# Reordering the seams of a Conformer block on one core: feed-forward work between queries and scores, softmax sums behind the values, two copies on VectorE

## The chip, the cores and the metric

The kernel runs on one core of a Trainium2 chip. The metric is the device time of one execution in microseconds (us), taken as the median of several executions. A kernel is set beside times of the kernel before on the same chip; some of these times are carried over from an earlier batch of runs. TensorE multiplies matrices, VectorE and ScalarE do elementwise work, GpSimd small jobs, and SyncE issues transfers. The profile writes them PE (with PEld for loading weights), DVE, ACT, POOL and SP.

## The reference

One Conformer block on two sequences of 4000 tokens, 512 features, bfloat16, cut to what matters here:

```python
h = _layernorm(x);   x1 = x + 0.5 * (_silu(h @ w_ff1_a) @ w_ff1_b)      # feed-forward 1, hidden 2048
h = _layernorm(x1);  q, k, v = h @ w_q, h @ w_k, h @ w_v
p = _softmax(einsum('btd,bsd->bts', q, k) * scale)                       # 4000 x 4000, one head of 512
x2 = x1 + einsum('bts,bsd->btd', p, v) @ w_o
h = _layernorm(x2) @ w_pw1;  h = h[..., :D] * _sigmoid(h[..., D:])       # gate
dc = depthwise_3_taps(h, dw);  dc = (dc - mean) / sqrt(var + 1e-05)      # mean, var over all tokens
x3 = x2 + _silu(dc) @ w_pw2
x4 = x3 + 0.5 * (_silu(_layernorm(x3) @ w_ff2_a) @ w_ff2_b)              # feed-forward 2
return _layernorm(x4)
```

## The kernel before

The tokens are cut into 16 chunks of 508 (the last of each sequence 444), each into four tiles of 127. The program is a list of stages: feed-forward 1 over all chunks, attention over all chunks with most of the convolution beside it, what is left of the convolution, feed-forward 2. Every engine runs its instructions in the order in which they are written; a wait is put in wherever a buffer is not ready. In `lags` wait pieces of work that TensorE does later (`pop` runs the oldest). Eight PSUM banks are used as two rings of four, S and Y. A bank is never read by two engines at once: the second reader waits for the first (`excl`).

The seam between feed-forward 1 and attention (DC is 4):

```python
for dc in range(DC):
    if dc == DC - 1:
        self.pop(1)              # a last piece of feed-forward 1
        old -= 1
    self.q_group(0, 0, dc)       # 4 matmuls, then a copy: ScalarE for even dc, VectorE for odd
# ... attention follows: scores of the first key tile need all four parts of the queries
```

The end of attention for the last chunk, and the convolution work that fills its layer norm:

```python
self.pop(3)
self.sums_direct(last % 2)       # 8 one-column matmuls on the split softmax sums, then 1/x on VectorE
self.pop(1)                      # the last values: 4 matmuls of 32 rows; then copy_o: output copies
# ...
self.conv_b(tail, DC - 3)
fill = [None, lambda: gates.append(self.conv_a(tail, DC - 3)), lambda: self.conv_b(tail, DC - 2),
        lambda: gates.append(self.conv_a(tail, DC - 2))]

def prepare(ti):
    self.project(last, ti)       # 4 matmuls on the output copies, then the residual on VectorE
    if ti == 2:
        gate("POOL")
    if fill[ti]:
        fill[ti]()
for ti in self.ln_tiles(last, ..., prepare, ("ACT", "ACT", "DVE", "DVE")):
    ...                          # cut: last gate of the convolution
gate("DVE")
drains = [self.depthwise(tail - 1, self.KEEP)]
for k in range(2):
    self.transpose_pair(k, 1, ("ACT", "DVE")[k], ybank(), last)
drains.append(self.depthwise(tail - 1, DC - 2))
```

The seam to feed-forward 2:

```python
finish(DC - 1, between)          # depthwise results of the last channel group; copies are put off
self.conv_shift(DC - 1)
self.swish(0, 3)
copy_away()                      # two copies out of PSUM, on ScalarE
# ... cut: weights
for cc in range(DC):
    self.swish(1, cc)            # ScalarE; TensorE's next 12 matmuls need them
self.pw2_x(0, all_t[2:], banks[2:])
self.pw2(0, all_t, banks, False)
x = [(ps[0:TILE, :], b_ps) for ps, b_ps in banks]
for ti in self.ln_tiles(0, ..., ("ACT", "ACT", "DVE", "DVE"), x):   # statistics on VectorE
    pass
# ... cut: pw2 of the second chunk, transposes of the first, then feed-forward 2
```

## Time and profile before

| | before |
|---|---|
| time, median of 3 runs | 2040.97 us (2040.7 to 2040.99) |
| span of the profiled execution | 2037.1 us |
| TensorE busy | 2028.9 us, all of the span |
| VectorE, ScalarE, GpSimd busy | 53%, 37%, 5% |
| TensorE's waits that the profile names | 2.0 us |
| granted TensorE clock | 1.00 |

Read it as a kernel whose only expensive thing is TensorE. VectorE at 53% is no limit on the average; it can matter only for a microsecond or two where one stage turns into the next. The change works on three such seams. Its lines are in the prediction.

### The profile page before, as it was taken

The numbers are of one execution on the slowest core, as the hardware profiler recorded it, in microseconds if no ns is written. First come the engines' busy times: TensorE is split into PE (matmuls) and PEld (weight loads), VectorE is DVE, ScalarE is ACT, GpSimd is POOL, SyncE is SP. The second block draws the span as 40 slices with busy tenths as digits, with TensorE's granted clock in tenths as the row PEclk, the third lists the DMA queues.
The fourth block names the chain that finished last, engine by engine and source line by source line (L and its number), as shares of the span: only waits on it lengthen the run. The fifth ranks groups of instructions, "written<-read, shape, count | busy, mean of one in ns | idle before, by whom it ended". The sixth has DMA issues, their size and how long they took to land.

```text
span 2037.1 us, 24581 instructions
## 1 busy us (share of the span) xinstructions
PE 2028.9 (100%) x9682; PEld 1030.5 (51%) x9682; DVE 1081.5 (53%) x2187; ACT 743.7 (37%) x1277; POOL 107.6 (5%) x235
## 2 busy tenths in 40 slices
PE   9999999999999999999999999999999999999998
PEld 5555555554444444445444444444455555555555
DVE  4234443334556667666766676667674443434433
ACT  3433333333333333333333333333345443443433
POOL 1000000000000000000000000000011000000000
PEclk9999999999999999999999999999999999999999
DMA  8122245420101111114421111111143111111111
GB/s 189 49 62 62 54 102 124 96 70 19 16 16 27 25 32 26 27 26 94 106 57 23 26 29 32 24 27 26 44 135 93 32 32 42 32 32 42 29 34 38
DMA packets 253122, 104.43 MB, mean 51 GB/s; under 512 B 193412, under 2 KB 252487, under 8 KB 252999
## 3 DMA queue, kind: packets, MB, share of 16 engines
q1 hardware_dynamic: 252321, 102.44, 21.6%
q8 instruction: 78, 1.28, 0.3%
q14 instruction: 45, 0.37, 0.1%
q10 hardware_dynamic: 678, 0.34, 0.1%
HBM read 33.77 MB, written 23.34 MB: 28 GB/s over the span
## 4 chain that ended last, share of the span: by engine, by line
PE 99%; ACT 0%; DVE 0%; issue 0%; POOL 0%; DVEq 0%
PE s L512 56%; PE y L512 42%; ACT work L562 0%; DVE wff L1215 0%; PE y L540 0%; ACT keys L562 0%; POOL work L1224 0%; DVE work L559 0%; DVE work L876 0%; PE y L527 0%; DVE wff L1102 0%; DVE work L1222 0%; ACT xt L562 0%; DVE work L835 0%; DVE work L1229 0%
## 5 line engine op out<-in xcount | busy, mean ns | idle before, releaser
L562 ACT ACTIVATE work<-s 128x508 bf16<-128x508 f32 (+3 forms) x1060 | 621.7, 587 | 1211.5 <-PE s L512 1207.1
L512 PE MATMUL s<-work,wff 128*128 128x508 bf16 (+4 forms) x2640 | 628.3, 369 | 0.8 <-ACT work L562 0.4
L512 PE MATMUL s<-work,keys 128*128 128x508 bf16 (+1 forms) x2048 | 516.6, 374 | 0.1
L512 PE MATMUL y<-work,keys 128*128 128x508 bf16 (+2 forms) x2048 | 503.9, 373 | 0.0
L512 PE MATMUL y<-wff,work 128*127 128x512 bf16 (+1 forms) x2000 | 501.4, 378 | 0.0
L959 DVE TENSOR_TENSOR work<-work 128x508 f32<-128x508 f32 (+2 forms) x496 | 334.4, 674 | 281.6 <-ACT work L562 280.8
L512 PEld LDWEIGHTS s<-work,wff 128*128 128x128 bf16 x2640 | 252.6, 98 | 277.0 <-issue 4.7
L512 PEld LDWEIGHTS y<-wff,work 128*127 128x127 bf16 x2000 | 274.4, 137 | 170.9
L512 PEld LDWEIGHTS s<-work,keys 128*128 128x128 bf16 x2048 | 199.4, 98 | 232.0 <-DVE work L876 0.6
L512 PEld LDWEIGHTS y<-work,keys 128*128 128x128 bf16 (+1 forms) x2048 | 193.6, 97 | 233.1 <-issue 6.2
L758 DVE SCALAR_TENSOR_TENSOR xt<-y,xt 127x512 bf16<-127x512 f32 x125 | 77.7, 682 | 364.0 <-PE y L512 364.0
L512 PE MATMUL s<-work 128*127 128x512 bf16 (+4 forms) x775 | 196.9, 378 | 1.2 <-DVE work L1333 1.2
L624 DVE BATCH_NORM_STATS2 work<-xt 127x6 f32<-127x512 bf16 x311 | 195.2, 676 | 5.2 <-DMA xt<-in_x_dram 4.9
L631 POOL TENSOR_TENSOR work<-work 127x4 f32<-127x4 f32 (+1 forms) x76 | 76.5, 1007 | 1129.4 <-DVE work L629 1129.4
L512 PEld LDWEIGHTS s<-work 128*127 128x127 bf16 (+2 forms) x775 | 94.8, 124 | 75.6 <-issue 4.0
L644 DVE TENSOR_SCALAR work<-xt,work 127x512 bf16<-127x512 bf16 x309 | 111.4, 406 | 27.4 <-POOL work L631 23.2
L758 DVE SCALAR_TENSOR_TENSOR xt<-s,xt 127x512 bf16<-127x512 f32 x55 | 38.0, 691 | 148.7 <-PE s L512 148.7
L758 DVE SCALAR_TENSOR_TENSOR xt<-s,work,xt 127x512 bf16<-127x512 f32 x64 | 48.0, 750 | 30.9 <-PE s L512 30.3
L1113 DVE SCALAR_TENSOR_TENSOR wff<-wff,s 128x508 bf16<-128x508 f32 (+1 forms) x57 | 38.7, 678 | 41.5 <-PE s L512 41.3
L562 ACT ACTIVATE wff<-s 128x508 f32<-128x508 f32 (+1 forms) x67 | 39.5, 591 | 53.5 <-PE s L512 53.4
L562 ACT ACTIVATE work<-keys,work 128x508 bf16<-128x508 bf16 (+1 forms) x68 | 52.3, 774 | 0.4 <-DVE work L1229 0.2
L1194 POOL COPY wff<-wff 128x1 bf16<-128x1 bf16 x56 | 10.4, 187 | 637.8 <-DVE wff L1113 635.0
(92 smaller groups left out, 413.0 us busy)
## 6 DMA issues: line engine op xcount, KB each, us to landing
keys<-keysd SPq DMA_DIRECT2D x62, 128.0 KB, 2.3
keysd<-work SPq DMA_DIRECT2D x14, 448.0 KB, 3.2
out_dram<-work SPq DMA_DIRECT2D x14, 448.0 KB, 3.2
dcvd<-wff SPq DMA_DIRECT2D x48, 127.0 KB, 1.9
keys<-dcvd SPq DMA_DIRECT2D x12, 508.0 KB, 4.9
xt<-in_x_dram SPq DMA_DIRECT2D x13, 448.0 KB, 4.8
wff<-in_w_ff_a_dram SPq DMA_DIRECT2D x15, 256.0 KB, 5.2
work<-work SPq DMA_TRANSPOSE x208, 2.5
```

What stands on the lines that cost most here:

```text
L512: self.S.op("PE", lambda e: e.matmul(out, lhsT, rhs, start=start, stop=stop, **kw), reads=reads, writes=[bank], inc=stop if inc is None el ...
L562: return self.S.op("ACT", lambda e: e.activation(out, in_, func, **kw), reads=reads, writes=writes)
L624: self.S.op("DVE", lambda e: e.bn_stats(self.st[sl][:, ti, 0:6], x), reads=[b_x], writes=[self.b_st[sl][ti]])
L631: S.op("POOL", lambda e: e.tensor_tensor(out=self.rs[sl][:, 0:n], in0=self.mv[sl][:, 0:n, 1], in1=self.neghalf[0:TILE, 0:n], op=ALU.pow), ...
L644: self.S.op("DVE", lambda e: e.tensor_scalar(out, x, self.mv[sl][:, ti, 0:1], self.rs[sl][:, ti:ti + 1], ALU.subtract, ALU.mult), reads=[b ...
L758: self.S.op("DVE", lambda e: e.scalar_tensor_tensor(out=self.XT[g][rows], in0=ps[rows], scalar=scalar, in1=self.XT[g][rows], op0=ALU.mult, ...
L959: S.op("DVE", lambda e, p=p, n=n, acc=acc: e.tensor_tensor(out=acc, in0=acc, in1=self.P[p][0:n, 0:W], op=ALU.add), reads=[self.b_P[p], sel ...
L1113: self.S.op("DVE", lambda e: e.scalar_tensor_tensor(out=out, in0=th, scalar=1.0, in1=ps[:, 0:W], op0=ALU.add, op1=ALU.mult), reads=[b_ps, ...
L1194: S.op("POOL", lambda e: e.tensor_copy(self.G[gs][:, jj, 0:1], self.G[gp][:, jj, CHUNK:CHUNK + 1]), reads=[self.b_G[gp][jj]], writes=[self ...
```

## The change

Its intent is to take single waits away from TensorE at the seams: more work between the last query group and the scores that need it; sums where their operands are long ready; the first tile's projection early, so that its layer norm starts early; and two copies moved to an idle VectorE so that ScalarE reaches the swishes sooner.

```diff
-                lambda: self.act(self.dcv[t][cc][:, 0:W], ps[:, 0:W], AF.Copy, [b_ps], [self.b_dcv[t][cc]]))
+                lambda eng="ACT": self.away(eng, self.dcv[t][cc][:, 0:W], ps[:, 0:W], b_ps, [self.b_dcv[t][cc]]))
 ...
         for dc in range(DC):
-            if dc == DC - 1:
-                self.pop(1)
-                old -= 1
             self.q_group(0, 0, dc)
+        self.pop(1)
+        old -= 1
 ...
         self.pop(3)
+        self.pop(1)
         self.sums_direct(last % 2)
-        self.pop(1)
 ...
-        self.conv_b(tail, DC - 3)
-        fill = [None, lambda: gates.append(self.conv_a(tail, DC - 3)), ...
+        fill = [lambda: self.conv_b(tail, DC - 3), lambda: gates.append(self.conv_a(tail, DC - 3)), ...
 ...
-            if fill[ti]:
-                fill[ti]()
+            fill[ti]()
 ...
-        def copy_away():
+        def copy_away(eng="ACT"):
             while copies:
-                copies.pop(0)()
+                copies.pop(0)(eng)
 ...
         self.swish(0, 3)
-        copy_away()
+        copy_away("DVE")
```

More of the change, by code (lines that the diff above doesn't have):

```diff
@@ L1457, in gate @@
             gates.pop(0)(eng)
-        fill = [None, lambda: gates.append(self.conv_a(tail, DC - 3)), lambda: self.conv_b(tail, DC - 2),
+        fill = [lambda: self.conv_b(tail, DC - 3), lambda: gates.append(self.conv_a(tail, DC - 3)), lambda: self.conv_b(tail, DC - 2),
                 lambda: gates.append(self.conv_a(tail, DC - 2))]
```

## The prediction

> **What bounds the kernel now.** I read the page first: what share of the span has TensorE, and at what clock.
>
> ```profile
> span 2037.1 us, 24581 instructions
> ## 1 busy us (share of the span) xinstructions
> PE 2028.9 (100%) x9682; PEld 1030.5 (51%) x9682; DVE 1081.5 (53%) x2187; ACT 743.7 (37%) x1277; POOL 107.6 (5%) x235
> ...
> PE 99%; ACT 0%; DVE 0%; issue 0%; POOL 0%; DVEq 0%
> ```
>
> TensorE is busy in all of the span, the granted clock reads 9 in all 40 slices, and the chain that ended last is TensorE for 99%. The change removes no matrix multiply, so only time in which TensorE stands still can be won. The list of TensorE's waits says how much there is of that:
>
> ```profile
> PE s L512 <- DVE work L1333: 1.2, 1, 1.2
> PE s L512 <- ACT work L562: 0.4, 1, 0.4
> PE y L540 <- ACT work L562: 0.2, 1, 0.2
> PE s L512 <- DVE work L559: 0.2, 1, 0.2
> ```
>
> That is 2.0 us in all, 1.6 of it at the start of the program, which the change doesn't touch. But ends of matmuls are modelled and overlap, so short stops hide in "busy". They show in the timeline as a distance between starts that is too long: in the steady stretches a 508- or 512-column matmul follows the last after 0.216 us (eight of 508 columns read 1.89 us, which is 7 x 0.216 plus a last one of 0.38). I looked for longer steps at the three places of the change. First, between the last feed-forward and the first scores (columns: start, duration, engine, line, operation, tiles, count, then idle time and releaser):
>
> ```profile
> 452.17 0.81 PE L512 MATMUL y<-wff,work 128*127 128x512 bf16 x3
> 452.82 1.03 PE L512 MATMUL s<-work 128*128 128x508 bf16 x4
> 453.68 2.19 PE L512 MATMUL s<-work,keys 128*128 128x508 bf16 x8
> ...
> 453.88 0.69 DVE L876 CAST work<-s 128x508 bf16<-128x508 f32 x1 [1.69 <-PE s L512]
> ```
>
> Eight score matmuls take 2.19 instead of 1.89 us. The fourth needs the last quarter of the queries, whose cast ends only at 453.88 + 0.69 = 454.57. So 0.30 us is lost here.
>
> Second, the end of attention:
>
> ```profile
> 1510.65 3.16 PE L512 MATMUL y<-work,keys 128*128 128x444 bf16 x16
> 1513.65 0.74 PE L512 MATMUL s<-work 128*127 128x1 bf16 x8
> 1514.32 0.37 PE L512 MATMUL y<-work,keys 32*128 32x444 bf16 x4
> ```
>
> The eight one-column sums, which wait for VectorE's split of the sums (its last instruction runs from 1513.53 to 1513.76), stand before the last four value matmuls.
>
> Third, the start of the second feed-forward (ScalarE's, VectorE's and TensorE's timelines, one after another):
>
> ```profile
> 1541.16 1.00 ACT L562 ACTIVATE keys<-y 128x444 bf16<-128x444 f32 x2
> 1542.05 2.90 ACT L562 ACTIVATE work<-keys,work 128x508 bf16<-128x508 bf16 x4
> ...
> 1541.78 0.70 DVE L624 BATCH_NORM_STATS2 work<-s 127x6 f32<-127x512 f32 x1 [1.37 <-PE s L512]
> ...
> 1542.91 2.96 PE L512 MATMUL y<-work 128*127 128x512 bf16 x12
> ```
>
> ScalarE copies two convolution results (1.00 us), then makes four swishes (2.90), and TensorE's twelve matmuls of the second chunk go at their pace: 2.96 us instead of 11 x 0.216 + 0.38 = 2.76. The transposes after them wait for ScalarE's normalizations (TensorE idle 0.25 us before 1546.35) and its copy out of a bank. Before its first statistics VectorE stands idle for 1.37 us.
>
> **What the Trainium skill says.** "TensorE: Matmul & The Clock Gate", in the section on 56 against 53.3 ns, gives N/2.4 + 2.5 ns per warm matmul, 216 ns for 512 columns; the trace agrees (0.216). "TensorEngine Tiling (Array Packing)", Key Properties, says that a change of tiling mode drains TensorE. The trace agrees: from the first of the four 32-row matmuls to the next work (1514.32 to 1514.62) pass 0.30 us, where one 444-column step takes 0.188. The change keeps two mode changes, so this cost stays. "ScalarE: Activation LUTs", What ACT_TABLE_LOAD costs, gives 186 ns + 0.833 ns per element, 93 more for each pointer operand, and an overlap of 93: a swish of 508 with two pointers would start every 0.70 us, as it does here. "VectorE: DVE Perf Modes", errata table, gives 120 + N cycles for a copy out of PSUM, 0.65 us for 508; the trace has 0.69 for such a cast, and I use that.
>
> **Part 1, feed-forward work between queries and scores.** The three matmuls at 452.17 move behind the fourth query group. That group then starts at 452.17, its cast 0.65 us earlier (453.23 to 453.92), while the scores still start at 453.68 and their fourth matmul at 453.68 + 3 x 0.216 = 454.33. The cast is done by then with 0.4 us to spare, so the stop goes: **-0.30 us**. The order of pops behind it is the same, so nothing is given back.
>
> **Part 2, the sums behind the values; the first tile's projection first.** Before, from the end of the 16 value matmuls (1510.65 + 16 x 0.188 = 1513.65) to the convolution's matmuls at 1514.62 is 0.97 us. After: mode change in 0.09 (what I found as the extra step at such places), the four matmuls with their drain 0.30, then eight sums without a wait at about 0.06 each, 0.48, then about 0.03: 0.90. So **-0.08 us**, give or take 0.05. The projection now comes straight after the sums, about 1514.55, and needs the output copies; the copies of the first 127 columns start when the values end, about 1514.11 (before, at 1514.71 on ScalarE and 1514.75 on VectorE), and the four of each engine take 1.10 and 1.28 us; by their sizes the first on each should be done by about 1514.45 and the second by about 1514.65; the third and fourth matmul need the second ones, at 1514.98 and 1515.2. No stop. Its residual waits for the reciprocal behind VectorE's four copies (1514.14 + 1.28 + 0.18, about 1515.6) and for its own matmuls (about 1515.6): equal. It starts 0.85 us earlier than before, which relieves the first two normalizations, but the fourth tile still follows its own projection, and the next stops of TensorE hang on that end:
>
> the convolution of the last chunk starts only when VectorE has copied the transposes (0.35 us lost near 1525.5), and the next depthwise bank waits for statistics and copy (0.24 near 1527.4). Both are chains from TensorE's own transposes and stay. The early projection is worth nothing more.
>
> **Part 3, two copies to VectorE.** The second swish group starts at 1541.16 instead of 1542.05: ScalarE's ends move to 1541.97, 1542.67, 1543.37, 1544.07, and TensorE needs them at 1542.87, 1543.52, 1544.17, 1544.81. So the twelve matmuls run at full pace, -0.25 us. Then VectorE becomes the limit. Its statistics from 1541.78, four normalizing steps to 1546.66, and the two copies of transposes (1.40) run one after another. The last norm ends 1546.66 as before; the last tile's transposes run to about 1546.95 instead of 1547.28; the two copies then end about 1548.09 instead of 1548.18, and the feed-forward can start at about 1548.14 instead of 1548.44: **-0.30 us**. VectorE's new copies take about 0.53 + 0.68 = 1.2 us, from 1540.4 to about 1541.65, in the idle 1.37 us. They just fit before 1541.78.
>
> **Sum.** 0.30 + 0.08 + 0.30 = 0.68 us off 2040.97: 2040.3. Everything later runs without a wait of TensorE, so a gain is kept to the end. The second copy of the program, for large scores, changes too but isn't run.
>
> **Rivals.** (a) VectorE is late: if its copies run past 1541.78 by x, statistics, norms and the start of the feed-forward move by x, as that chain has no slack left. For it: only 0.1 us of margin. Against: their banks were read long before, so nothing holds them. A miss of 0.3 would undo part 3: 2040.6. (b) The projection right behind the sums stops for the output copies, which one convolution group of 0.86 us covered before, and the earlier residual is held by the reciprocal behind the copies: a stop of up to 0.3 us, 2040.6; together with (a) 2040.9. (c) The early start helps more than I think: if the late residuals cause the stops at 1525.5 and 1527.4, up to 0.59 more comes off, 2039.7. Against it: the trace names the copies and statistics behind TensorE's own transposes there. (d) Weights arriving late for the earlier feed-forward: the last quarter of the first matrix is landed by 1545.3, three us before, so no.
>
> **Range and chances.** The three times of before lie within 0.3 us, the parts are certain to about 0.2 each, (c) sets the lower end and (a) with (b) the upper: 2039.6 to 2040.9. A change of 2% is 41 us; all of TensorE's waits are 2.0 us and the places of the change hold under 2. Faster 0.004, same 0.993, slower 0.003.
>
> **What would show it.** Part 1: eight score matmuls in 1.89 us behind the queries. Part 2: the sums right behind the 32-row matmuls, no step over 0.3 us up to the second projection, the steps of 0.56 and 0.42 us near 1525 and 1527 unchanged. Part 3: twelve matmuls in 2.76 us, statistics starting as soon after the first tile's matmuls as now, the last transposes following VectorE's norm. Wrong if one of these steps is longer than before, or if a new stop turns up after the feed-forward has started.

## The result and the profile after

The changed kernel takes 2040.7 us in the median of 4 runs (2040.1 to 2041.36), the kernel before 2040.98 of 4 runs (2040.7 to 2041.0; three of the four are those of the table above). The ratio is 0.9999, with a 95% interval from 0.9982 to 1.0016: the same.

The page after, the lines that answer to those of before:

```profile
span 2037.0 us, 24582 instructions
## 1 busy us (share of the span) xinstructions
PE 2028.8 (100%) x9682; PEld 1030.8 (51%) x9682; DVE 1082.9 (53%) x2189; ACT 743.1 (36%) x1275; POOL 107.7 (5%) x235
...
PE 99%; DVE 0%; ACT 0%; issue 0%
```

The two copies have changed engines (VectorE 2187 to 2189 instructions, ScalarE 1277 to 1275), and the span is 0.1 us shorter. From the page one would say that nothing happened. TensorE's list of waits (releaser, us in total, times, longest):

```profile
PE s L512 <- DVE work L1333: 1.2, 1, 1.2
PE s L512 <- ACT work L562: 0.6, 1, 0.6
PE s L512 <- DVE work L559: 0.2, 1, 0.2
PE s L512 <- issue: 0.2, 1, 0.2
```

The wait of the transposes for ScalarE at line 540 is gone. The second line grew from 0.4 to 0.6 us. It lies in the first 8 us of the program, where the diff changes nothing. The last line is no new stop: before has the same long step in front of the same convolution group (0.498 us at 1496.17, here 0.510 at 1496.32), with an idle time just short of what the list shows. More of it under e0. Now the three places. TensorE's and VectorE's timelines at the first:

```profile
452.18 1.46 PE L512 MATMUL s<-work 128*128 128x508 bf16 x6
453.48 0.81 PE L512 MATMUL y<-wff,work 128*127 128x512 bf16 x3
454.13 1.88 PE L512 MATMUL s<-work,keys 128*128 128x508 bf16 x8
...
453.68 0.69 DVE L876 CAST work<-s 128x508 bf16<-128x508 f32 x1 [1.04 <-PE s L512]
```

The query groups run through, the three feed-forward matmuls stand behind them, and the eight score matmuls take 1.88 us instead of 2.19: the last cast ends at 454.37, 0.41 us before the fourth of them (454.78) needs it. The start of the scores is 0.45 us later than before, which has nothing to do with this place: everything in this execution is 0.45 us late from the first chunk on. TensorE's timeline at the second place (a row gathers instructions of one name; here the seven are the last three full value matmuls and the four of 32 rows, and the twelve are the eight sums and the first projection):

```profile
1513.23 1.02 PE L512 MATMUL y<-work,keys 128*128 128x444 bf16 x7
1514.19 1.55 PE L512 MATMUL s<-work 128*127 128x1 bf16 x12
```

The sums follow the values, and the projection follows the sums without a gap that the timeline would split. The third place, in ScalarE's, VectorE's and TensorE's timelines, and behind them VectorE's copies of the transposes, first before and then after:

```profile
1540.52 3.62 ACT L562 ACTIVATE work<-keys,work 128x508 bf16<-128x508 bf16 x5 [0.25 <-DVE work L1229]
...
1540.40 1.21 DVE L559 CAST keys<-y 128x444 bf16<-128x444 f32 x2
1541.85 0.70 DVE L624 BATCH_NORM_STATS2 work<-s 127x6 f32<-127x512 f32 x1 [0.24 <-PE s L512]
...
1542.95 2.75 PE L512 MATMUL y<-work 128*127 128x512 bf16 x12
1545.54 1.65 PE L540 MATMUL y<-work 127*128 127x127 bf16 x16
```

```profile
1546.78 1.40 DVE L559 COPY work<-y 128x1016 bf16<-128x1016 bf16 x2
```

```profile
1546.66 1.28 DVE L559 COPY work<-y 128x1016 bf16<-128x1016 bf16 x2
```

Five swishes now follow one another on ScalarE. VectorE has the two copies in 1.21 us and still stands idle for 0.24 us before its statistics. The twelve matmuls take 2.75 us, not 2.96, and the sixteen transposes 1.65 us; before, they were spread from 1545.71 to 1547.45. (At this place the trace of after runs 0.08 us behind that of before.)

So each place is better, and the span shows 0.1 us of it. To see where the rest went, cut the execution at starts of TensorE's instructions that every version has: the small 3x3 matmuls for the convolution's taps in feed-forward 1 (T), the first matmuls of 32 rows (R, end of the first chunk's attention), the first transposes of the last chunk (X), the first matmul of feed-forward 2 (F), and the last matmul (L). Each stretch is one start taken from the next:

| stretch, us | before | after | difference |
|---|---|---|---|
| begin to T | 44.652 | 45.095 | +0.443 |
| T to R (part 1) | 471.054 | 470.744 | -0.310 |
| R to X (part 2) | 1008.203 | 1008.148 | -0.055 |
| X to F (part 3, and what part 2 leaves) | 24.536 | 24.129 | -0.407 |
| F to L | 482.800 | 482.800 | 0.000 |
| L to end | 5.902 | 6.035 | +0.133 |
| span | 2037.147 | 2036.951 | -0.196 |

The four stretches in the middle give -0.772 us, against a forecast of -0.68. The two ends, in which nothing was changed, took 0.576 back.

### The profile page after: what moved, and what is told of

Its sections match the earlier page's. It is cut to its first block, busy times and chain, and to the rows that moved or that the text cites. A ratio compares the mean times of both kernels' runs of the same rounds, so it can differ in the third digit from the quotient of the medians.

```text
span 2037.0 us, 24582 instructions
## 1 busy us (share of the span) xinstructions
PE 2028.8 (100%) x9682; PEld 1030.8 (51%) x9682; DVE 1082.9 (53%) x2189; ACT 743.1 (36%) x1275; POOL 107.7 (5%) x235
## 3 DMA queue, kind: packets, MB, share of 16 engines
q8 instruction: 78, 1.28, 0.3%
## 4 chain that ended last, share of the span: by engine, by line
PE 99%; DVE 0%; ACT 0%; issue 0%
PE s L512 57%; PE y L512 43%; DVE work L624 0%; ACT work L562 0%; PE y L540 0%; DVE work L559 0%; PE y L527 0%; DVE wff L1215 0%; ACT keys L562 0%; DVE wff L1102 0%; DVE work L726 0%; ACT xt L562 0%; DVE work L835 0%; DVE work L1331 0%; DVE work L836 0%
```

## The experiments

State of the theory: the change wins about 0.77 us, all of it in the parts that it touches, and the ends of the execution vary from run to run by as much. The rivals: the changed kernel has an unsteadiness of its own; the gain seen in one trace is an accident; or the parts gain through one another. All ten experiments gave correct results. In the table, the stretches of their profiled executions (us), and the medians of their times with the number of runs. The median of the kernel before beside them was 2041.56 for e0 to e3, 2041.36 for e4, e5, e6 and e7 (nine of its ten times are those of the first batch), and 2041.88 for e4b and e8, which ran on another chip. All runs were fast but the single one of e4b, whose state is unknown; its stretches that the edit doesn't touch equal those of before within 0.002 us, so its trace can be used. T to R and F to L, equal on both chips, say the same of e8's.

| kernel | begin to T | T to R | R to X | X to F | F to L | L to end | median (runs) |
|---|---|---|---|---|---|---|---|
| before | 44.652 | 471.054 | 1008.203 | 24.536 | 482.800 | 5.902 | 2040.98 (4) |
| after | 45.095 | 470.744 | 1008.148 | 24.129 | 482.800 | 6.035 | 2040.70 (4) |
| e0: before again | 45.265 | 471.054 | 1008.562 | 24.544 | 482.800 | 6.331 | 2041.81 (5) |
| e1: part 1 | 44.523 | 470.744 | 1008.215 | 24.540 | 482.800 | 5.595 | 2040.64 (5) |
| e2: part 2 | 44.854 | 471.055 | 1008.155 | 24.547 | 482.800 | 5.428 | 2041.35 (5) |
| e3: part 3 | 44.525 | 471.054 | 1008.212 | 24.138 | 482.800 | 6.343 | 2040.87 (5) |
| e4: sums alone | 44.944 | 471.055 | 1008.353 | 24.535 | 482.800 | 5.664 | 2041.64 (4) |
| e4b: projection alone | 45.242 | 471.055 | 1008.678 | 24.537 | 482.800 | 5.792 | 2041.90 (1) |
| e5: after again | 44.675 | 470.744 | 1008.144 | 24.126 | 482.800 | 6.516 | 2040.79 (5) |
| e6: copies twice | 44.945 | 470.741 | 1008.154 | 24.922 | 482.800 | 5.503 | 2041.42 (4) |
| e7: other engines | 44.563 | 470.744 | 1008.431 | 24.304 | 482.800 | 6.360 | 2040.56 (6) |
| e8: transposes first | 45.731 | 470.744 | 1007.501 | 24.178 | 482.800 | 6.110 | 2040.24 (5) |

### e0: the kernel before against itself

No edit.

> The kernel before, unchanged, against itself. My theory: the change won about 0.77 us on TensorE after the first feed-forward chunk's start, and the clock's warm-up at the start of the program (in the trace after, 13 slow warm-up matmuls instead of 11, and everything behind 0.45 us late) hides it in single times. If so, this kernel against itself spreads by about 0.5 to 1.3 us between executions though nothing differs, its trace has 1.68 us from the first transposes' place to the sums exactly as before (stretches after the start equal to those of before within 0.02 us), and only the start differs. Rival: times of before are steady to 0.3 us, as its four runs suggested, and the changed kernel is less steady for a reason of its own; then this one spreads by 0.3 us at most.

(The clause with 1.68 us in this text is a slip; it answers to no quantity, and I don't use it.)

Measured: 2041.36 to 2042.59 over its 5 runs, and 2040.77 to 2042.43 for the same program as "before" in the same rounds, 9 runs; ratio 1.0001. The same program thus spreads by over 1.6 us between executions, more than the 1.3 that I had expected at most, and its median was 0.25 us off itself. The rival falls: the 0.3 us within which the first four runs of before lay were luck. The ends do vary: begin to T 45.265 against 44.652, L to end 6.331 against 5.902. But my reason for the start was only half of it. TensorE's timelines of the first microseconds, first the changed kernel's, then this one's:

```profile
1.18 5.63 PE L512 MATMUL s<-work 128*128 128x508 bf16 x13 [1.18 <-DVE work L1333]
```

```profile
1.18 5.23 PE L512 MATMUL s<-work 128*128 128x508 bf16 x13 [1.18 <-DVE work L1333]
...
8.51 0.62 PE L512 MATMUL s<-work,wff 128*128 128x127 bf16 x8 [0.49 <-DMA wff<-in_w_ff_a_dram]
```

The thirteen warm-up matmuls of 508 columns go at 0.42 us each until the clock is released (the traces' clock records put this at 4.41 us in e1 to 7.13 in e4b), then at 0.215. In the changed kernel's trace all thirteen were slow and the first transposes too, in this one only eleven, as in the first trace of before. This execution is late for another reason: it waited 0.49 us for the first weights. Over the twelve traces 8 to 13 of the thirteen are slow, as "TensorE: Matmul & The Clock Gate", What's actually happening, says of such counts: the window in which the release is decided runs freely, so the number differs from run to run. But the start, 44.52 to 45.73 us, doesn't follow that number alone (8 slow ones in e1, which has the shortest start, and in e8, which has the longest). The traces tell what it does follow: in all twelve, T comes 36.75 to 36.76 us after the ninth matmul of the first feed-forward. In eight of them this matmul starts 0.04 to 0.05 us after the second piece of its weights has landed (at 7.72 us in e1, at 8.93 in e8). In the other four (before, e3, e4b, e6) the weights were there already, and the chain of warm-up matmuls, transposes and copies came last. At the other end, the last output transfer is issued 2.4 us after L in all traces, and the execution ends 3.0 to 4.1 us (5.43 to 6.52 less that) later, when the transfer has landed.

Not expected either: R to X was 0.36 us longer than in before. TensorE stands 0.35 us near 961 us, in front of a convolution group, and the profile names no releaser ("issue"). The same stop shows near 960 us in e4 (0.24) and e7 (0.29) and in no other trace. The group waits for several semaphores, among them those of transposing transfers that bring its input. TensorE's and SyncE's timelines in this trace:

```profile
961.51 1.24 PE L512 MATMUL s<-work,wff 128*128 128x508 bf16 x5 [0.18 <-issue]
...
957.51 2.52 SPq L570 DMA_TRANSPOSE work<-work x2
```

The second of the two transposes is issued at 958.77 and lands 2.50 us later, at 961.26; the group starts 0.246 us behind that. In e4 and e7 it is 0.247 and 0.246 us as well. In the nine traces without the stop the last transpose had landed 0.39 to 0.80 us before the group's turn. So the stop is a late transfer, and "issue" on the list hides it. The same holds near 1496: there the group starts 0.245 to 0.247 us after the last landing in all twelve traces, with a step of about 0.51 us where 0.188 is usual. This stop of about 0.31 us is as large as part 1's gain, and neither the prediction nor any version here touches it. The stop near 960 touches the reading of part 2 alone, where I take it off.

### e1, e2, e3: each part alone

The edits, shortened (e3 also has the new lambda for the copy, as in the change):

```diff
  e1 (on the kernel before)              e2 (on the kernel before)             e3 (on the kernel before)
-     if dc == DC - 1: pop(1) ...      -  self.sums_direct(last % 2)         -  copy_away()
+ self.pop(1) behind the loop          -  self.pop(1)                        +  copy_away("DVE")
                                       +  self.pop(1)
                                       +  self.sums_direct(last % 2)
                                       -  self.conv_b(tail, DC - 3) before the tiles
                                       +  fill[0] = the same, behind the first projection
```

> Part 1 alone: the three feed-forward matmuls behind the fourth query group. Theory: the stop of 0.30 us in the first scores goes and nothing else moves: from the taps' small matmuls to the first 32-row matmuls 0.31 us less than before, later stretches equal within 0.02 us. Rival: the gain depends on the other parts or is given back at the first exponentials, then less than 0.2 us. The time: 0.3 us less, inside the spread.

> Part 2 alone: sums behind the values and the first projection ahead of the convolution. Theory: 0.06 us less from the first 32-row matmuls to the last chunk's transposes, and the two stops behind these (0.35 and 0.24 us in before) stay, so from the transposes to the second feed-forward the same 24.54 us as before within 0.03. Rival: the earlier residuals relieve VectorE behind the transposes, then 0.1 us or more less there, and the 0.10 us by which that stretch did better than I had predicted belongs to this part.

> Part 3 alone: two copies on VectorE. Theory: the whole gain between the transposes and the second feed-forward is this part's: 0.41 us less there (24.13 instead of 24.54), and the earlier stretches equal to before. Rival: 0.30 us less as I had predicted, the rest being part 2's.

Measured: e1 has T to R 470.744, exactly the changed kernel's, and every later stretch within 0.012 us of before. e2 has R to X 0.048 us shorter; X to F stays at 24.547 against 24.536. e3 has X to F 24.138, 0.398 us shorter, and the earlier stretches of before. So the parts add up without touching one another: -0.310 - 0.048 - 0.398 = -0.756, against -0.772 with all three. The rival that part 2 helps behind the transposes falls: alone it changes nothing there. The early start of the layer norm, which was part of its intent, is worth nothing.

Their times don't resolve this. e1's median is 0.92 us under before's of the same rounds, where its trace gains 0.31; the ratios are 0.9997, 1.0000 and 0.9998, each with an interval of about 0.0014 either way, some 2.8 us.

### e5: the changed kernel again

No edit.

> The changed kernel again, with five rounds. Theory: the trace's stretches behind the start equal those of the first run within 0.02 us (0.77 us less than before in all), and the median of its times is 0.3 to 1.0 us under before's, depending on how the warm-ups fall. Rival: the gain seen in one trace is an accident of that execution; then the stretches differ by more than 0.1 us.

Measured: the middle stretches are 470.744, 1008.144, 24.126 and 482.800, at most 0.004 us off the first trace. The gain is no accident. Median 2040.79 against 2041.36, 0.57 us less; ratio 0.9996, interval 0.9982 to 1.001.

### e6: the two copies made twice

```diff
 def copy_away(eng="ACT"):
+    again = list(copies) if eng == "DVE" else []
     while copies:
         copies.pop(0)(eng)
+    for copy in again:
+        copy(eng)
```

> The changed kernel with the two VectorE copies made twice (1.2 us more on VectorE before its statistics, same values). It measures how much room the copies have. Theory: in the changed kernel VectorE stands idle for 0.24 us between the second copy and the first statistics, and from the statistics on it has almost no slack, so the second feed-forward starts later by 1.2 - 0.24 = about 1.0 us, less up to 0.15 us of slack behind. Rival: TensorE's own matmuls or ScalarE bound this stretch and VectorE has slack; then under 0.5 us later.

VectorE's timeline:

```profile
1540.26 2.33 DVE L559 CAST keys<-y 128x444 bf16<-128x444 f32 x4
1542.51 0.69 DVE L624 BATCH_NORM_STATS2 work<-s 127x6 f32<-127x512 f32 x1
```

The four copies take 2.33 us, 1.12 more than two, and the statistics follow without a gap. In the changed kernel they start 1.45 us after the first copy (1541.85 - 1540.40), here 2.25: 0.80 us later. X to F is 0.793 us longer (24.922 against 24.129). So behind the statistics there is no slack at all, and in front of them 0.24 us. The rival falls; I had been 0.2 us high, mostly because I forgot that instructions without a wait between them overlap: the added copies took 1.12 us, not 1.2, and the statistics start 0.08 us before the last copy ends.

### e4 and e4b: the halves of part 2

e4 takes only the exchange of sums and last values, e4b only the projection ahead of the convolution (both on the kernel before).

> Of part 2 only the sums behind the values, the convolution still ahead of the first projection. Theory: the values' end and the output copies are the same as in the change, and the convolution's matmuls cover the copies, so the small stop of 0.03 us in the first projection goes: from the 32-row matmuls to the transposes 0.06 to 0.10 us less than before. The projection being later by one group of 0.86 us changes nothing behind. Rival: the earlier projection is what gains; then nothing or little is won here.

> Of part 2 only the first projection ahead of the convolution, the sums still before the last values: the case of my rival b, with nothing between the values and the projection. Theory: the projection must wait for the output copies, 0.28 us from the values' end plus the way of a semaphore, so TensorE stops 0.4 to 0.5 us and the stretch from the 32-row matmuls' neighbourhood to the transposes gets longer than before by about that. Rival: no stop, then equal to before within 0.05.

e4: R to X is 1008.353, but with the 0.24 us of the unexplained stop; without it about 0.09 us less than before, so a little more than part 2 as a whole wins. e4b's timeline of TensorE at the projection:

```profile
1515.65 1.08 PE L512 MATMUL s<-work 128*127 128x512 bf16 x4 [0.36 <-ACT work L562]
```

TensorE stands idle for 0.36 us until ScalarE's first output copy, and R to X is 0.475 us longer than before. This is my rival (b), and it is real where nothing stands between the values and the projection. In the change the eight sums stand there, about 0.5 us, and the step to the second projection matmul is only 0.03 us too long (0.246 us). What makes it so the trace doesn't name: the copy that it reads had ended 0.1 us before its weights were loaded. So of the halves only the sums behind the values gain. The projection ahead takes 0.03 to 0.04 us of that back, and without the sums in front of it costs 0.475.

### e7: the transposes copied by other engines

```diff
-    self.transpose_pair(k, 1, ("ACT", "DVE")[k], ybank(), last)
+    self.transpose_pair(k, 1, ("DVE", "ACT")[k], ybank(), last)
...  # the last tile of the second pair:
-    self.away(eng, lin[:, 1, :, 0:TAIL], ...)
+    self.away("DVE", lin[:, 1, :, 0:TAIL], ...)
```

> The changed kernel with the last chunk's transposes copied by other engines: the first pair on VectorE, of the second pair the first tile on ScalarE and the last on VectorE. Theory: the stop of 0.36 us of the last chunk's convolution hangs on VectorE's two copies one after another; shared by two engines they end 0.1 to 0.2 us sooner, the stop shrinks to about 0.2, and as the bank's statistics and copy follow VectorE's end, the second stop stays at about 0.24: the stretch from the transposes to the second feed-forward is 0.1 to 0.2 us shorter. Rival: the stop hangs on the norms or on residuals, then unchanged; or ScalarE's copy is the later one, then longer.

X to F got 0.175 us longer (24.304 against 24.129). VectorE's timeline:

```profile
1524.39 0.69 DVE L559 COPY work<-y 128x1016 bf16<-128x1016 bf16 x1
1525.47 0.29 DVE L559 COPY work<-y 128x252 bf16<-128x252 bf16 x1 [0.39 <-ACT work L562]
```

VectorE is done with the first pair at 1525.08 and then waits 0.39 us for ScalarE, because both halves of the second pair lie in one bank and the kernel lets only one engine at a time read it. The copies ran one after another as before, the first of them on the slower path: 0.60 us on ScalarE and 0.29 on VectorE, where VectorE alone needs 0.76 for both. The expectation failed on a rule that stands in the kernel's own bookkeeping. That the stop of TensorE follows this end is confirmed: its step there grew by the same 0.17 us. The second stop didn't shrink for it (steps of 0.422 and 0.425 us), so it hangs on the first.

### e8: transposes ahead of the depthwise matmuls

```diff
         gate("DVE")
-        drains = [self.depthwise(tail - 1, self.KEEP)]
         for k in range(2):
             self.transpose_pair(k, 1, ("ACT", "DVE")[k], ybank(), last)
+        drains = [self.depthwise(tail - 1, self.KEEP)]
         drains.append(self.depthwise(tail - 1, DC - 2))
```

> The changed kernel with one line moved: the three depthwise matmuls that stood before the last chunk's transposes now stand behind them. Theory: the two stops left there (0.36 us for VectorE's copies of the second pair, 0.24 for a bank of the depthwise results) are a chain that begins with the last norm, and TensorE reached the second pair's transposes about 0.5 us after that norm; with the transposes earlier by 0.65 us of work and that work behind them, the copies end before TensorE comes, and the later depthwise takes the bank of the first pair, long free. So from the first 32-row matmuls to the second feed-forward 0.4 to 0.6 us less than the changed kernel's 1032.27. Rival: the transposes now wait for the norms or the copies stand behind VectorE's gate multiplication, then under 0.2 us less. The times: below the changed kernel's and before's, on the whole 1.2 us under before, about the size of the spread.

TensorE's timeline, the changed kernel and then this one (whose clock readings are 0.64 us late at R, from its long start):

```profile
1525.98 1.66 PE L512 MATMUL s<-work,wff 128*128 128x444 bf16 x8 [0.19 <-DVE work L559]
1527.72 0.82 PE L512 MATMUL y<-wff 128*128 128x508 bf16 x3
```

```profile
1524.88 1.55 PE L512 MATMUL y<-wff 128*128 128x508 bf16 x6
1526.26 1.66 PE L512 MATMUL s<-work,wff 128*128 128x444 bf16 x8
1527.76 0.81 PE L512 MATMUL y<-wff 128*128 128x508 bf16 x3
```

The six depthwise matmuls now stand between the transposes and the convolution that needs their copies, the idle 0.19 us in front of it is gone, and the next depthwise group starts 1.50 us after the convolution's start instead of 1.74. From R to F it takes 1031.679 us against 1032.277: 0.598 us less, at the upper end of what was expected. Both stops that the prediction had found near 1525.5 and 1527.4 are gone with one line. For the first, the cause is that the transposes are issued earlier and other work stands behind them. For the second, the line does two things, which e8 doesn't separate: the chain starts sooner, and the later depthwise group takes another bank, that of the first pair.

From T to L this version has 1985.223 us, the changed kernel 1985.821 and the kernel before 1986.593. Its median is 2040.24 us (2039.73 to 2040.99) against 2041.88 (2040.66 to 2042.41) for before in the same rounds, ratio 0.9993, interval 0.9979 to 1.0007. By the trace it beats both kernels, by 0.60 and 1.37 us. By the times it is still "the same".

## Why the prediction was right or wrong

- **The whole.** 2040.3 was forecast, 2040.7 measured, inside the range and inside 2%. The sum of parts was right to 0.1 us: -0.68 against -0.772 in the trace, -0.756 from the parts alone. What puts the measured median 0.4 us above the forecast is not a part of the change. That the median fell inside the range was in part luck: beside the median of before in e8's rounds, 2041.88, the same gain of 0.77 would have given 2041.1, outside.
- **Part 1** was right in mechanism and size: -0.30 against -0.310, and e1 shows that nothing else moves.
- **Part 2** was right in mechanism: -0.08 against -0.055 (e2: -0.048). Its own terms give 0.97 - 0.90 = 0.07, not 0.08. The term that was mis-sized is the projection straight behind the sums: "No stop" was a step 0.03 us too long, and e4 without it wins about that more. The statement that the early projection is worth nothing more is shown by e2.
- **Part 3** was right in mechanism and mis-sized: -0.30 against -0.407 (e3: -0.398). The step that failed is "the two copies of transposes (1.40) run one after another", which was to hold the feed-forward until 1548.14. The 1.40 of before was not all work: its second copy had waited about 0.11 us for the last transposes. After, the copies took 1.28 us, nothing stood between them and the norm, and they ended at 1547.94, before TensorE was done with its own five matmuls behind the transposes (1548.12). In the clock of before, 0.08 us earlier, these are 1547.86 and 1548.04, against a forecast of 1548.09 and 1548.14. What binds is VectorE's chain from its statistics to the last norm, and behind it TensorE's own transposes and matmuls: the last four transposes start 0.06 us after that norm's end (1546.80 and 1546.74), and e6 shows that a delay of 0.80 us in this chain delays the feed-forward by 0.79.
- **Rival (a)**, a late VectorE, did not happen: the margin was 0.24 us, not 0.1. **Rival (b)** needs the sums elsewhere, as e4b shows. **Rival (c)** fell with e2: residuals that come sooner don't touch the stops at 1525.5 and 1527.4. e8 shows what does. **Rival (d)**, late weights, did not happen: the feed-forward starts 0.215 us after the matmul before it.
- **The range** rested on "The three times of before lie within 0.3 us". This was the weakest step. The profiled execution of before, 2041.11 us, lay outside them already, and the same program ranged over more than 1.6 us in e0. The range held the median, but single runs of the changed kernel went to 2041.36. "A gain is kept to the end" is true up to the last matmul (F to L is 482.800 us in all twelve traces); the transfer behind it varies by 1.1 us.

What stays open: why the same transfers come sooner or later from one execution to the next, at the start, near 960 us and at the end.

## What to carry to other kernels

When an engine is busy all the time, look for stops in the distance between the starts of its instructions, not in its busy share, and judge sub-microsecond changes by stretches between fixed instructions of the trace: here these repeat to about 0.01 us, but for the stop near 960 us in three traces, where the times of one program spread by over 1.6 us. Where the profile gives a stop to "issue", look at when the transfers that feed the instruction landed. In e8 a chain across engines was shortened at its head, by issuing the first link earlier and putting independent work behind it. Before giving half of a job to a second engine, ask whether the two share a bank, and whether what follows has slack for it.

## What the Trainium skill lacked or had wrong

- "TensorE: Matmul & The Clock Gate", Back-to-back issue gap, gives about 131 ns per matmul of 512 columns, and 81 ns at 128, as the sustained rate of a stream with weight loads, and calls the formula of 216 ns too high there. Here the stream with a weight load for each matmul runs at 216 ns for 508 to 512 columns, and the transposes of 127 columns at about 56 ns (four in 0.22 us). The formula agrees with this kernel and the sustained figures don't.
- "TensorEngine Tiling (Array Packing)", Key Properties, says that a change of mode drains TensorE, without a cost. Here it is about 0.10 us into the mode of 32 rows and 0.10 out of it (0.284 and 0.286 us between starts where 444 columns take 0.187).
- "VectorE: DVE Perf Modes", errata table, gives 120 + N cycles for a copy out of PSUM, 0.65 us for 508 fp32 columns; measured were 0.68 to 0.69. Its section "The DRAIN you can't avoid" says that the next operation does not start until the pipe is empty, and adds that one that is not held starts earlier, without a figure. Two copies with no wait between them took 1.21 us, with durations of 0.615 and 0.678: the profile's start of the second lies 0.085 us ahead of the first one's end. Without this overlap the margin in front of the statistics, 0.24 us, would have been about 0.16.
- "TensorE: Matmul & The Clock Gate", What's actually happening, tells that the count of slow matmuls varies from run to run, which the traces here show too (8 to 13). None of the pages that I used gives a figure for what the two ends together do to one program's time. Here: 1.2 us in the start (clock release and first weights) and 1.1 us in the landing of the last transfer.
